# A recurrent attention and SoLU kernel on one core: chunk outputs copied aside, score matmuls in another order, masks moved

## The chip, the core and the metric

The kernel runs on one core of one Trainium2 chip. The metric is the device time in microseconds (us) of one execution. Before the change it is 380.94 us, the median of three runs (380.69 to 381.0).

## The reference

Gated linear attention over 4 batches, 8 heads, 768 steps and a head width of 48, followed by a feed-forward block over the 3072 tokens of width 384, with 1024 hidden units:

```python
for t in range(S):
    state = alpha[:, :, t, :, None] * state + np.einsum('bhd,bhe->bhde', k[:, :, t], v[:, :, t])
    y[:, :, t] = np.einsum('bhd,bhde->bhe', q[:, :, t], state)
...
h = x @ w_in
e = np.exp(h - np.max(h, axis=-1, keepdims=True))
solu = h * (e / (np.sum(e, axis=-1, keepdims=True) + 1e-09))
ln = (solu - mean) / np.sqrt(var + 1e-06) * g_ln
return (ln @ w_out).astype(np.float32)
```

`x` is `y` with its heads laid side by side; `mean` and `var` are those of `solu` along the hidden units. The weights `w_in` and `w_out` come as 64-bit floats and are converted on the chip.

## The kernel before

**Tiling.** The 768 steps are cut into six chunks of 128 (`G` = 6, numbered from 0). A chunk of all four batches is one unit of work, 512 tokens in the feed-forward block. Attention of a chunk: running products of alpha by scans on VectorE (`scan_back` L206, `scan_on` L215); keys and queries multiplied by them; scores of key against query (`scores` L271, TensorE into PSUM); the scores times a triangular mask, into `sT` in SBUF (`masked` L285, VectorE); the values read with these (`read_values` L349) on top of what the carried state gives (`read_state` L341), both into one PSUM bank per batch; a copy to `x` by ScalarE (L356). The state is decayed by GpSimd (`decay` L255, line L261) and added to (`next_state` L358).

**Rows of a head.** A head's 48 rows stand as 32 "first" rows and 16 "last" rows. The last rows of two heads share a block, so the queries of a block are copied twice by ScalarE, each time with the other head's rows at zero (`apart` L243, line L245). A score is two matmuls added in PSUM: one of first rows, one of last rows. `scores` issues, for each of four heads of a half, the first rows of four batches and then the last rows of four batches. Four banks `a0` to `a3`, one per batch, hold a half's scores; they are also used by the turned inputs, by the values and by other small products, in the order of the program.

**Feed-forward.** For each chunk `up` (L379) makes 128 hidden units at a time: three matmuls into a bank `h` (L387), Exp on ScalarE (L401), the product `h * e` on VectorE (L402), which also frees the bank, and its square on ScalarE (L403). `running` (L406) adds `e` on GpSimd and the square on VectorE (L418). `down` (L492) takes a batch of 128 tokens: eight matmuls of 385 columns into one of the two banks `o` (L498), in two halves; the last column gives the sum. `finish` (L503) computes a scale from that sum (L516 to L521 on VectorE, a power on GpSimd at L529), for chunk 0 also adds a mean (L525), scales on ScalarE (L531) and sends the rows to DRAM over SP's queue (L532).

**What sets the order.** There is no scheduler: each engine runs its instructions in the order in which the Python code issues them, and a wait holds up what stands behind it. The first part of the program is written out by hand: loads and turned inputs of chunk 0 (L670 to L695), scores and masks of chunk 0 (L696 to L702), then chunk 0's `up` steps among the conversion of the weights on VectorE (`bits` L581, lines L590 to L602, which reads what `fetch` L550 loads at L561), then chunk 0's `down` steps among the attention of chunk 1 (L742 to L812). SP's queue carries nearly all transfers, among them `move_lasts` and `move_firsts` (L227, L234), which bring queries and decays to the place where `read_state` and `decay` want them. From L816 on, a table says at which of the eight `up` steps of a chunk which part of the next chunk's attention is issued: `head` ahead of `up`, `behind` after it and ahead of `running`, `middle` after `running`, `tail` after the `down` step that is due. The table `first` holds for chunk 1's `up` steps, during which chunk 2's attention runs and no `down` is due; `usual` holds for the others.

Of the kernel before, what the change touches and what calls it, by code (L numbers as in the profile page):

```python
# [32 lines left out]
def fast_path(ctx, tc, q, k, v, alpha, moe_w_in, moe_w_out, moe_g_ln, out):  # L33
# [231 lines left out]
    def quarter(b):  # L265
        return slice(32 * b, 32 * b + 32)
# [4 lines left out]
    def scores(g, half, a=None):  # L271
        a = a or banks("a", [NP, P])
        for i in range(NP):
            h = half * NP + i
            for kb, qb in ((h, h), (H + h // 2, H + h)):
                for b in range(B):
                    nc.tensor.matmul(  # L277
                        a[b][:, i], lhsT=kT[quarter(b), kb], rhs=qv[quarter(b), qb, 0:P], start=kb == h, stop=kb != h,
                        tile_position=(32 * b, 0), skip_group_check=True,
                    )  # L280
        masks[half] = a
# [3 lines left out]
    def masked(half, batches=range(B)):  # L285
        a = masks[half]
        for b in batches:
            nc.vector.tensor_tensor(  # L288
                out=sT[:, b, half * NP : half * NP + NP], in0=a[b], in1=mask[:, None, :].to_broadcast([P, NP, P]),
                op=ALU.mult,  # L290
            )

    def keys_back(g, t=None):
# [198 lines left out]
    def down(n, half, part=range(HF)):  # L492
# [4 lines left out]
        for f in (half * HF + i for i in part):  # L497
# [3 lines left out]
            )  # L501

    def finish(n):  # L503
        g, b = divmod(n, B)
        d = st[n]
        s, o = sums[:, n], d["o"][:, 0:DM]
        t0 = b * S + g * P
        if g == G - 1:
# [6 lines left out]
            return  # L515
        nc.vector.tensor_copy(out=s[:, 0:1], in_=d["o"][:, DM : DM + 1])  # L516
        t = small.tile([P, 1], FP, name="t")
# [4 lines left out]
        if g == 0:  # L522

            o = work.tile([P, DM], FP, name="o_mean")
            nc.vector.scalar_tensor_tensor(  # L525
                out=o, in0=mean_sb, scalar=s[:, 0:1], in1=d["o"][:, 0:DM], op0=ALU.mult, op1=ALU.add
            )
        r = small.tile([P, 1], FP, name="r")
        nc.gpsimd.tensor_tensor(out=r, in0=s[:, 3:4], in1=mhalf, op=ALU.pow)  # L529
# [154 lines left out]
    scan_on(0, 0)  # L684
    t = three("tp_q", [(ps_o, "o"), (ps_o, "o"), (ps_a, "a0")])
    turned(qn, ends_of(qn, 3), t)
    for i in (2, 0, 1):
        if i == 1:
            scan_on(0, i)
        part = slice(NP * i, NP * i + NP)  # L690
        nc.vector.tensor_tensor(  # L691
            out=qe[:, :, 0:P] if i == 2 else qv[:, part, 0:P], in0=t[i], in1=aT[:, part, 1:SW], op=ALU.mult
        )
        if i == 2:
            apart()  # L695
    warm(2, ps_a, "a1")  # L696
    scores(0, 0)
    t = [x.tile([P, NP, P], FP, tag=n, name="a_" + n) for x, n in ((ps_h, "h"), (ps_o, "o")) for _ in range(2)]
    scores(0, 1, t)
    read_begin()  # L700
    masked(0)
    masked(1)  # L702
    bits(0)
# [60 lines left out]
    down(0, 1)  # L764
    mean(1)
    alpha_over(1)
    load(alpha, an, 2)
    tq += three("tp_q2", [(ps_h, "h")])
    turned(qn, ends_q, tq, range(H, NB))
    load(q, qn, 2)  # L770
    down(1, 1)
    keys_back(1, three("tp", [(ps_a, "a2"), (ps_a, "a3"), (ps_h, "h")]))
    scan_on(1, 2)
# [3 lines left out]
    move_lasts()  # L777
    finish(0)
    in_range(7)
# [6 lines left out]
    scores(1, 0)  # L786
    finish(1)
    decay(1)
    masked(0)
    down(2, 1)  # L790
    scores(1, 1)
    masked(1)
    finish(2)
    alpha_T(2)
    down(3, 0)
# [7 lines left out]
    for i in range(3):  # L803
# [5 lines left out]
    down(3, 1, (2, 3))  # L809
    finish(3)  # L810
    scan_on(2, 2)
# [10 lines left out]
    first = dict(  # L822
        head={3: "keys_back", 5: "masked0", 6: "masked1"},
        behind={0: "v", 1: "on1", 2: "lasts firsts", 3: "apart", 5: "decay", 7: "alpha back"},
        middle={7: "read1 values over"},
        tail={4: "scores0", 5: "scores1", 6: "begin read0"},
    )
# [60 lines left out]
    for g in range(1, G + 1):  # L888
# [6 lines left out]

        after = None
        if not rise:
# [520 lines left out]
```

## Time and profile before

| | |
|---|---|
| median of three runs | 380.94 us |
| the profiled execution, its own time | 380.75 us |
| its span, first to last instruction | 378.9 us |
| granted clock of TensorE, mean | 0.998 |
| busy VectorE, ScalarE, GpSimd | 246.0, 144.7, 120.5 us |
| `up` matmuls, L387 | 133.4 us |
| `down` matmuls, L498 | 133.6 us |
| score matmuls, L277 | 24.8 us, 704 records |
| value and state matmuls, L326 | 22.9 us |
| masks, L288 | 44 of 683 ns |

A page of the profile gives for each group of instructions the line, engine, operation, what is written from what, sizes and count, then busy time, the mean of one, and the idle time of the engine ahead of them with what ended it. A timeline row gives start and duration in us from the span's start, engine, line, what is written from what, and the number of records merged in the row; in brackets stands the idle time ahead of it and who ended it. PE is TensorE, PEld its loading of weights, DVE VectorE, ACT ScalarE, POOL GpSimd; SP issues transfers. A matmul of 32-bit floats leaves two records. Some matmul records are missing from a trace. A record's duration includes a tail that overlaps with the next record: where a row of many is followed at once by another, the distance between their starts tells what it cost.

### The profile page before, as it was taken

The numbers are of one execution on the slowest core, as the hardware profiler recorded it, in microseconds if no ns is written. First come the engines' busy times: TensorE is split into PE (matmuls) and PEld (weight loads), VectorE is DVE, ScalarE is ACT, GpSimd is POOL, SyncE is SP. The second block draws the span as 40 slices with busy tenths as digits, with TensorE's granted clock in tenths as the row PEclk, the third lists the DMA queues.
The fourth block names the chain that finished last, engine by engine and source line by source line (L and its number), as shares of the span: only waits on it lengthen the run. The fifth ranks groups of instructions, "written<-read, shape, count | busy, mean of one in ns | idle before, by whom it ended". The sixth has DMA issues, their size and how long they took to land. (4 is left out here: it accounts for less than half of the span.)

```text
span 378.9 us, 10022 instructions
## 1 busy us (share of the span) xinstructions
PE 362.4 (96%) x4337; PEld 215.1 (57%) x4337; DVE 246.0 (65%) x377; ACT 144.7 (38%) x256; POOL 120.5 (32%) x127
## 2 busy tenths in 40 slices
PE   8789899989999999999999999999999999999994
PEld 8675335656654665555665556565556565555552
DVE  1899878996998879855666855756965314434500
ACT  3628566681255235252341252441341142332101
POOL 7000000010246990775111765112683211333200
PEclk9999999999999999999999999999999999999999
DMA  9982968149149704836033545004041000000011
GB/s 182 189 315 89 210 205 210 43 93 194 59 107 187 172 8 98 155 87 152 22 85 76 114 104 133 24 3 106 0 112 43 24 15 8 22 22 21 27 42 49
DMA packets 72439, 36.06 MB, mean 95 GB/s; under 512 B 48184, under 2 KB 69952, under 8 KB 72384
## 3 DMA queue, kind: packets, MB, share of 16 engines
q1 hardware_dynamic: 71360, 34.39, 38.9%
q10 hardware_dynamic: 1024, 0.92, 0.7%
q8 instruction: 36, 0.59, 0.7%
q14 instruction: 19, 0.16, 0.1%
HBM read 25.30 MB, written 4.72 MB: 79 GB/s over the span
## 5 line engine op out<-in xcount | busy, mean ns | idle before, releaser
L387 PE MATMUL h<-x,w_in 128*128 128x512 f32 x288 | 133.4, 601 | 3.4 <-DVE room L402 2.1
L498 PE MATMUL o<-w_out,room 128*128 128x385 f32 x384 | 133.6, 492 | 0.9 <-DVE o_mean L525 0.9
L498 PEld LDWEIGHTS o<-w_out,room 128*128 128x128 f32 x384 | 71.1, 189 | 55.7 <-issue 13.8
L387 PEld LDWEIGHTS h<-x,w_in 128*128 128x128 f32 x288 | 52.4, 189 | 62.7 <-issue 47.7
L402 DVE TENSOR_TENSOR room<-h,e 128x512 f32<-128x512 f32 x40 | 27.6, 690 | 61.1 <-ACT e L401 61.1
L401 ACT ACTIVATE e<-h 128x512 f32<-128x512 f32 x40 | 23.8, 596 | 96.0 <-PE h L387 95.8
L418 POOL TENSOR_TENSOR p<-p,e 128x512 f32<-128x512 f32 x30 | 41.1, 1369 | 27.6 <-ACT e L401 27.2
L403 ACT ACTIVATE u<-room 128x512 f32<-128x512 f32 x40 | 25.2, 630 | 36.4 <-DVE room L402 36.4
L529 POOL TENSOR_TENSOR r<-sums,mhalf 128x1 f32<-128x1 f32 x20 | 12.2, 608 | 78.4 <-DVE sums L521 78.2
L288 DVE TENSOR_TENSOR sT<-a,mask 128x512 f32<-128x512 f32 x44 | 27.3, 683 | 14.8 <-PE a L277 14.8
L418 DVE TENSOR_TENSOR p<-p,u 128x512 f32<-128x512 f32 x30 | 24.2, 807 | 8.6 <-ACT u L403 8.6
L204 DVE TENSOR_TENSOR_SCAN hT<-aT,unit 128x516 f32<-128x516 f32 x18 | 22.3, 1285 | 7.8 <-ACT aT L674 7.7
L277 PEld LDWEIGHTS a<-qv,kT 32*128 32x128 f32 x704 | 21.9, 186 | 8.7 <-POOL p L418 1.6
L277 PE MATMUL a<-qv,kT 32*128 32x128 f32 x704 | 24.8, 278 | 1.8 <-DVE qv L691 0.8
L212 POOL COPY fend<-hT 128x12 f32<-128x12 f32 x6 | 4.1, 680 | 69.9 <-DVE hT L204 69.9
L204 DVE TENSOR_TENSOR_SCAN aT<-aT,seed 128x516 f32<-128x516 f32 x18 | 25.4, 1442 | 0.2
L326 PE MATMUL y<-sT,vn 128*32 128x128 f32 x768 | 22.9, 274 | 1.0 <-DVE sT L288 0.8
L326 PEld LDWEIGHTS y<-sT,vn 128*32 128x32 f32 x768 | 20.9, 110 | 4.3 <-issue 3.1
L225 POOL TENSOR_TENSOR kT<-kT,hT 128x1024 f32<-128x1024 f32 (+1 forms) x8 | 13.3, 1682 | 22.8 <-DVE kT L179 22.8
L196 ACT ACTIVATE sq<-an,mone 128x1536 uint8<-128x1536 f32 x12 | 18.9, 1574 | 0.2
L531 ACT ACTIVATE o_sb<-o,r 128x384 f32<-128x384 f32 x16 | 9.3, 582 | 24.1 <-POOL r L529 24.1
L356 ACT COPY x<-y 128x384 f32<-128x384 f32 x24 | 11.2, 478 | 14.4 <-PE y L326 14.2
(142 smaller groups left out, 366.0 us busy)
## 6 DMA issues: line engine op xcount, KB each, us to landing
vn<-in_v_dram SPq DMA_DIRECT2D x24, 192.0 KB, 4.3
an<-in_alpha_dram SPq DMA_DIRECT2D x20, 192.0 KB, 4.6
out_dram<-o_sb SPq DMA_DIRECT2D x20, 192.0 KB, 1.9
room<-in_moe_w_in_dram SPq DMA_DIRECT2D x6, 512.0 KB, 7.8
room<-in_moe_w_out_dram SPq DMA_DIRECT2D x8, 384.0 KB, 3.9
kn<-in_k_dram SPq DMA_DIRECT2D x16, 192.0 KB, 4.4
qn<-in_q_dram SPq DMA_DIRECT2D x16, 192.0 KB, 4.9
lot<-qe SPq DMA_DIRECT2D x40, 64.5 KB, 2.1
```

What stands on the lines that cost most here:

```text
L196: nc.scalar.activation(out=sq, in_=x, func=AF.Relu, scale=sign, bias=mone, accum_out=over[:, g, i : i + 1])
L204: nc.vector.tensor_tensor_scan(out=o, data0=a, data1=s, initial=1.0, op0=ALU.mult, op1=ALU.add)
L225: nc.gpsimd.tensor_tensor(out=kT[:, part], in0=kT[:, part], in1=hk[:, part], op=ALU.mult)
L277: nc.tensor.matmul(a[b][:, i], lhsT=kT[quarter(b), kb], rhs=qv[quarter(b), qb, 0:P], start=kb == h, stop=kb != h, tile_position=(32 * b, 0 ...
L288: nc.vector.tensor_tensor(out=sT[:, b, half * NP : half * NP + NP], in0=a[b], in1=mask[:, None, :].to_broadcast([P, NP, P]), op=ALU.mult,)
L326: nc.tensor.matmul(y_bank(b)[quarter(r), a], lhsT=lhsT, rhs=rhs, start=(b, r) not in begun, stop=stop, tile_position=(row, 32 * r), skip_g ...
L387: nc.tensor.matmul(h, lhsT=w_in[:, a, f * P : (f + 1) * P], rhs=d["x"][:, a].rearrange("p b t -> p (b t)"), start=(a == 0), stop=(a == KC ...
L401: nc.scalar.activation(out=e, in_=h, func=AF.Exp)
L402: nc.vector.tensor_tensor(out=u, in0=h, in1=e, op=ALU.mult)
L403: nc.scalar.activation(out=u2, in_=u, func=AF.Square)
L418: eng.tensor_tensor(out=p, in0=d[0][i] if f == 1 else p, in1=d[f][i], op=ALU.add)
L498: nc.tensor.matmul(d["o"][:, 0 : DM + 1], lhsT=u_of(g, f)[:, b * P : b * P + P], rhs=w_out[:, f], start=(f == 0), stop=(f == FC - 1), skip ...
```

## The change

Seven edits go together:

- **Queries in needed order.** In the prologue the query blocks are turned in the order 0 to 3, 8 to 11, 4 to 7 instead of 0 to 11, and the products follow in that order (0, 2, 1 instead of 2, 0, 1). The two warm-up matmuls ahead of the scores go; four are put ahead of the turn of the queries.
- **Scores by first rows.** `scores` issues all first rows of a half ahead of all last rows, and takes heads in the order 0, 2, 1, 3. This holds for all six chunks. Only a bank's very first matmul carries `start`.
- **Two masks off VectorE.** In chunk 0 the mask of the last batch of each half is made by a ScalarE copy from PSUM and a GpSimd product in place.
- **Copied chunks.** The outputs of chunk 0's batches 0 and 1 are copied by ScalarE from their banks into SBUF (`hold`), into a part of `lot` that is free by then; their `finish` reads the copy, and comes later: after the first and the second masks of chunk 1 instead of after `move_lasts` and after the first scores.
- **`alpha_T(2)`** is issued ahead of the second half of chunk 1's scores and masks instead of after `finish(2)`.
- **`finish(3)`** comes after the first `up` of chunk 1 instead of before the scans of chunk 2.
- **Masks ahead of a sum.** In chunk 1's `up` steps 4 and 5 the scores and masks of chunk 2 are both issued right after `up`, ahead of that step's `running`, instead of the scores at the end of the step and the masks at the head of the next.

```diff
     def scores(g, half, a=None):
         a = a or banks("a", [NP, P])
-        for i in range(NP):
-            h = half * NP + i
-            for kb, qb in ((h, h), (H + h // 2, H + h)):
+        for last in range(2):
+            for i in (0, 2, 1, 3):
+                h = half * NP + i
+                kb, qb = (H + h // 2, H + h) if last else (h, h)
                 for b in range(B):
                     nc.tensor.matmul(
-                        a[b][:, i], lhsT=kT[quarter(b), kb], rhs=qv[quarter(b), qb, 0:P], start=kb == h, stop=kb != h,
+                        a[b][:, i], lhsT=kT[quarter(b), kb], rhs=qv[quarter(b), qb, 0:P], start=not last and not i, stop=bool(last),
...
+    def masked_apart(half, b):
+
+        x = sT[:, b, half * NP : half * NP + NP]
+        nc.scalar.copy(out=x, in_=masks[half][b])
+        nc.gpsimd.tensor_tensor(out=x, in0=x, in1=mask[:, None, :].to_broadcast([P, NP, P]), op=ALU.mult)
...
+    def hold(n):
+
+        a = 2 * H * SW + (DM + 1) * (n % 2)
+        st[n]["held"] = lot[:, a : a + DM + 1]
+        nc.scalar.copy(out=st[n]["held"], in_=st[n]["o"][:, 0 : DM + 1])
+
     def finish(n):
...
-        s, o = sums[:, n], d["o"][:, 0:DM]
+        s, whole = sums[:, n], d.get("held", d["o"])
+        o = whole[:, 0:DM]
...
-    t = three("tp_q", [(ps_o, "o"), (ps_o, "o"), (ps_a, "a0")])
-    turned(qn, ends_of(qn, 3), t)
-    for i in (2, 0, 1):
+    t = three("tp_q", [(ps_a, "a0"), (ps_o, "o"), (ps_o, "o")])
+    warm(4, ps_a, "a1")
+    turned(qn, ends_of(qn, 3), t, (*range(NP), *range(H, NB), *range(NP, H)))
+    for i in (0, 2, 1):
...
-    warm(2, ps_a, "a1")
     scores(0, 0)
...
-    masked(0)
-    masked(1)
+    for half in range(2):
+        masked(half, range(B - 1))
+        masked_apart(half, B - 1)
...
     mean(1)
+    hold(0)
     alpha_over(1)
...
     down(1, 1)
+    hold(1)
     keys_back(1, three("tp", [(ps_a, "a2"), (ps_a, "a3"), (ps_h, "h")]))
...
     move_lasts()
-    finish(0)
     in_range(7)
...
     scores(1, 0)
-    finish(1)
     decay(1)
     masked(0)
+    finish(0)
+    alpha_T(2)
     down(2, 1)
     scores(1, 1)
     masked(1)
+    finish(1)
     finish(2)
-    alpha_T(2)
     down(3, 0)
...
     down(3, 1, (2, 3))
-    finish(3)
     scan_on(2, 2)
...
     first = dict(
-        head={3: "keys_back", 5: "masked0", 6: "masked1"},
-        behind={0: "v", 1: "on1", 2: "lasts firsts", 3: "apart", 5: "decay", 7: "alpha back"},
+        head={3: "keys_back"},
+        behind={
+            0: "v", 1: "on1", 2: "lasts firsts", 3: "apart", 4: "scores0 masked0", 5: "scores1 masked1 decay",
+            7: "alpha back",
+        },
+        tail={6: "begin read0"},
         middle={7: "read1 values over"},
-        tail={4: "scores0", 5: "scores1", 6: "begin read0"},
     )
...
-        after = None
+        after = 3 if g == 1 else None
```

More of the change, by code (lines that the diff above doesn't have):

```diff
@@ L515, in finish @@
             return
-        nc.vector.tensor_copy(out=s[:, 0:1], in_=d["o"][:, DM : DM + 1])
+        nc.vector.tensor_copy(out=s[:, 0:1], in_=whole[:, DM : DM + 1])
         t = small.tile([P, 1], FP, name="t")
@@ L522, in finish @@
         if g == 0:
-            o = work.tile([P, DM], FP, name="o_mean")
+            centred = work.tile([P, DM], FP, name="o_mean")
             nc.vector.scalar_tensor_tensor(
-                out=o, in0=mean_sb, scalar=s[:, 0:1], in1=d["o"][:, 0:DM], op0=ALU.mult, op1=ALU.add
+                out=centred, in0=mean_sb, scalar=s[:, 0:1], in1=o, op0=ALU.mult, op1=ALU.add
             )
+            o = centred
         r = small.tile([P, 1], FP, name="r")
```

## The prediction

> **What bounds the kernel now.** I read the page first, for which engine fills the span, then the waits of TensorE, then the timeline of TensorE around each wait, then the other engines' timelines at the same moments. The page:
>
> ```profile
> span 378.9 us, 10022 instructions
> ...
> PE 362.4 (96%) x4337; PEld 215.1 (57%) x4337; DVE 246.0 (65%) x377; ACT 144.7 (38%) x256; POOL 120.5 (32%) x127
> ```
>
> TensorE is the bound, so only its idle or slowed time can be won. Its waits, longest groups first (time, times, longest):
>
> ```profile
> PE h L387 <- DVE room L402: 2.1, 4, 0.9
> PE tp_q L164 <- DMA qn<-in_q_dram: 1.4, 1, 1.4
> ...
> PE o L498 <- DVE o_mean L525: 0.9, 1, 0.9
> PE a L277 <- DVE qv L691: 0.8, 1, 0.8
> PE y L326 <- DVE sT L288: 0.8, 1, 0.8
> ...
> PE h L387 <- DVE g_col L614: 0.7, 1, 0.7
> ```
>
> All lie before 143.2 us; from there to 373.8 us TensorE has no gap over 0.02 us. So the change can win only in the prologue (0 to 31), chunk 0's down stage (70 to 98) and chunk 1's up stage (113 to 143). Busy time hides more: TensorE's timeline in that last stage,
>
> ```profile
> 122.19 0.54 PE L277 MATMUL a<-qv,kT 32*128 32x128 f32 x8
> 123.04 2.01 PE L277 MATMUL a<-qv,kT 32*128 32x128 f32 x56 [0.32 <-ACT qv L245]
> 124.98 2.84 PE L387 MATMUL h<-x,w_in 128*128 128x512 f32 x6
> 127.76 3.44 PE L277 MATMUL a<-qv,kT 32*128 32x128 f32 x64
> 131.12 2.84 PE L387 MATMUL h<-x,w_in 128*128 128x512 f32 x6
> ```
>
> and the same 64 score records where nothing disturbs them:
>
> ```profile
> 172.65 2.07 PE L277 MATMUL a<-qv,kT 32*128 32x128 f32 x64
> 174.65 2.84 PE L387 MATMUL h<-x,w_in 128*128 128x512 f32 x6
> ```
>
> From start to next start: 2.79 and 3.36 us against 2.00. So 0.79 and 1.36 us are lost there, of which the list of waits shows 0.32.
>
> **What the Trainium skill says.** Perfetto Trace Analysis, "Identifying the Most-Contended Engine": busy matmul time is no good measure of TensorE, because its instructions overlap. The trace agrees: 3.44 against 2.07 us for equal work. PSUM — Partial Sum Buffer, "The four PSUM rules": the first matmul of a group clears written-bits of its whole bank, not data, so the new order may carry `start` on the first of a bank alone. No row prices this. GPSIMD Engine Reference, "8. Key points": it cannot read PSUM, which is why a ScalarE copy comes first. SBUF — State Buffer, "SBUF: two separate sides": a VectorE operation with two SBUF inputs and a reading GpSimd operation exclude each other. The trace agrees: L518 takes 1.29 us beside the key products, 0.16 alone. The masks have one SBUF input, and take 0.60 each.
>
> **Prologue.** Before, both query products wait for the whole turn: qe at 17.67, qv at 18.27, scan 18.87, last product 20.13. Now the first block is turned first. It is ready at about 15.9, but the scan holds VectorE to 16.80; so qv at 16.84, qe 17.45, scan 18.04, last product 19.30 to 19.99, all by 0.60 to 1.2 us a step from the old rows. ScalarE's two copies (L245) end at 18.9 and 19.5. TensorE: two warm-up matmuls (0.7 us) go from the path; four now stand in the 1.41 us wait for q, where 8 records at 0.13 plus a tail of 0.2 fit (13.4 to 14.6); were they late, the scan would hide it. First-row scores run 17.65 to 18.7, the last rows behind the copies to 20.1, the second half to 22.1. The first masks begin at 20.27 (before 21.20), three instead of four; the second half's at 22.17, so VectorE is free at 24.05 instead of 26.0.
>
> The two masks taken off it: ScalarE copy 0.6 us (as L674, 0.59), GpSimd product between 1.09 (L253) and 2.23 (the first L418 of a chunk); I take 1.29. The second ends at 24.1, at the high end 26.0 with the first queued ahead. Its reader, batch 3 of the values, comes up at 25.3: free, or 0.7 late. Values end at 26.2 (before 28.3), key turns at 27.9.
>
> This lead is not kept. The next thing on the path is VectorE's weight conversion, which sets `up` 0:
>
> ```profile
> 25.99 0.95 DVE L590 TENSOR_SCALAR lot<-room 128x768 uint32<-128x768 uint32 x1
> ...
> 29.55 0.96 DVE L602 TENSOR_TENSOR w_in<-lot 128x768 f32<-128x768 f32 x1
> 30.43 0.16 DVE L614 TENSOR_SCALAR g_col<-tp_g 128x8 f32<-128x8 f32 x1
> ```
>
> It needs three slices of w_in, and in the trace the third lands at 24.80; SP issues it at 17.39, nothing in the change moves that. So it starts at 24.85, not 24.05, and wins 25.99 - 24.85 = **1.14 us**, and TensorE waits some 1.6 us for it (27.9 to 29.5), which also covers the 0.7. From here to 82 us VectorE and ScalarE form one chain (the L402 waits) and loads follow its releases, so 1.14 is carried on. If the landing moves, so does this: I keep 0 to 1.5.
>
> **Held chunks (70 to 98), in old times less 1.14.** Two finishes leave VectorE's scan chain: each 0.97 us (82.83 - 81.86). `down(2,0)` no longer waits 0.89 for a bank; the second scores wait for L783, which ends at 85.68 instead of 86.65: TensorE gains 0.98. The two holds cost ScalarE 0.48 us each (row L356), 0.38 apart when back to back. The first delays the alpha check and with it the reload of alpha and all behind it on SP's queue by 0.4; the second delays the key copies by 0.1, which wait for TensorE anyway. Out of that queue goes one output ahead of `move_firsts` (0.6 us of issue). Net: the last move lands about 0.2 to 0.3 earlier. That matters, as the old row shows:
>
> ```profile
> 95.32 1.70 POOL L261 TENSOR_TENSOR state<-state,lot 128x384 f32<-128x384 f32 x2 [7.59 <-DMA lot<-qv]
> ```
>
> The second decay ended at 97.02, the state reads went on at 97.08. TensorE now comes at 95.3, the masks' last bank is free at 96.4 (the alpha transposes, 2.9 us, now stand ahead of the second masks), but the decay ends near 96.8. So of 0.98 + 0.31 only **0.28** stays; bounds -0.3 to 0.7. Queued behind: finishes 0 to 2 go through GpSimd after the decay, and the third's ScalarE output waits for the first output to land (issue 98.1 plus 1.9 = 100.0), with the copies of x behind it, which start at 101.5. Covered by 1 us, and by 2 more before `up` 0 would notice. The third `finish` behind `up` leaves VectorE's queue, where it took 3.2 us (106.82 to 110.05); L402 no longer makes `up` 2 wait: **0.31**.
>
> **Chunk 1's up stage.** First rows first: by my count ScalarE's copies end 0.2 and 0.6 before their scores come up, so the 0.79 goes. Masks ahead of the sum: the first masks start at TensorE's last score instead of after
>
> ```profile
> 125.50 1.19 DVE L418 TENSOR_TENSOR p<-p,u 128x512 f32<-128x512 f32 x1 [0.70 <-ACT u L403]
> 126.62 2.47 DVE L288 TENSOR_TENSOR sT<-a,mask 128x512 f32<-128x512 f32 x4
> ```
>
> They end about 0.15 before the second scores need the last bank: 1.36 goes. What is late next: the decay before the state reads. Its transfers follow twelve loads and move by 0.28 only; landing at 129.2, decay to 130.4 or 130.8. TensorE wants it at 131.46: slack 0.7. So **2.15**, bounds 1.0 to 2.2. The last wait there, 0.60 for x (L356), stays.
>
> **Sum.** 1.14 + 0.28 + 0.31 + 2.15 = 3.88 us. The profiled run took 380.75 (span 378.9 and 1.85 around it): 376.87. The median of the runs is 0.19 above it, 380.94, giving 377.06. I say 377.0. With every bound low, 0 - 0.3 + 0.31 + 1.0 = 1.0: 379.9; with every bound high, 1.5 + 0.7 + 0.31 + 2.2 = 4.7: 376.2.
>
> **Rivals.** *Gate of the weights.* The landing or VectorE's masks slip past 26.0 and the prologue gives nothing: 380.94 - 2.74 = 378.2. For it: all queues are 88% busy in the first 31 us. Against: the landing doesn't depend on the changed engines. *Gate of the decay.* In chunk 1 the transfers or GpSimd's queue, full from 120.7 to 141.4, end last, and about 1.3 of the 2.15 is given back: 378.4. For it: slack of only 0.7. Against: its products start earlier too. Both together: 379.7. *It does nothing*, because every wait is replaced: 380.9; against, the sums above would have to fail in three separate stages. *The scores themselves become slower.* Each first and last row now lie sixteen matmuls apart, in all twelve score groups; no wait covers it in the eight of chunk 1's up stage and later. At 0.49 us each the 3.88 is gone; at 0.7, 380.94 - 3.88 + 5.6 = 382.7, slower. Against: the values, also started once a bank, take 28 ns a record (3.63 / 128), the scores 31; four row groups still alternate as before.
>
> **Chances.** Forecast (376.2 to 377.8) 0.63; gate of the weights 0.11; of the decay 0.14; both 0.04; nothing 0.04; slower scores 0.04. Range 376.0 to 379.0: it leaves out both gates at once, nothing and slower, 0.12, and something at the edges. About 0.2% (0.76 us) is what a measurement can tell from no change: faster 0.92, same 0.04, slower 0.04.
>
> **What would show it.** Right: first L590 near 24.9 with VectorE idle ahead of it, `up` 0 at 29.5; a wait of about 1 us before the state reads near 95; two score groups of 2.0 us in chunk 1; no gap after about 140. Wrong: `up` 0 still near 30.6; score records over 31 ns in late chunks; state reads of chunk 1 waiting for L261; batch 3 of the values waiting for GpSimd by more than the 1.6.

## The result and the profile after

The changed kernel takes 378.33 us (median of seven runs, 377.24 to 379.79) against 380.69 us in the same session: a ratio of 0.9941, 95% interval 0.9928 to 0.9953, so faster by 2.4 us. The forecast was 377.0. Run again in a later session, unaltered, it took 377.22 us (five runs, 376.36 to 378.06), ratio 0.9902 (0.9888 to 0.9916), while the kernel before stayed at 380.7 to 381.0. Repeats of the changed kernel thus differ by more than one session's interval tells. Where variants are compared below, differences under about 1 us are read from the traces and not from the times. A trace is one execution, and shows where the time went in that one.

The profiled execution took 378.33 us. Its page:

```profile
span 376.5 us, 10033 instructions
...
PE 363.0 (96%) x4341; PEld 215.8 (57%) x4341; DVE 246.2 (65%) x375; ACT 147.1 (39%) x260; POOL 124.8 (33%) x129
```

The span is 2.36 us shorter (378.89 to 376.53 unrounded), as much as the executions differ (380.75 to 378.33). TensorE's busy time grew by 0.6 us although its work is the same but for two more warm-up matmuls, so the gain isn't seen there. Its waits, with the same columns as before:

```profile
PE h L394 <- DVE room L409: 1.6, 3, 0.9
PE h L394 <- DVE g_col L629: 1.1, 1, 1.1
...
PE y L333 <- POOL state L261: 0.9, 1, 0.9
PE y L333 <- issue: 0.6, 2, 0.5
PE h L394 <- ACT x L363: 0.6, 1, 0.6
...
PE y L333 <- DVE sT L289: 0.2, 1, 0.2
```

The waits for a bank of `down` (L525 before) and for `sums` are gone, that for the first masks fell from 0.8 to 0.2. The wait for `state` grew from 0.3 to 0.9, and "issue", time in which TensorE waited for nothing that the profile names, from 0.2 to 0.6.

The prologue, in VectorE's timeline:

```profile
23.45 0.68 DVE L289 TENSOR_TENSOR sT<-a_o,mask 128x512 f32<-128x512 f32 x1
25.18 0.95 DVE L605 TENSOR_SCALAR lot<-room 128x768 uint32<-128x768 uint32 x1 [1.05 <-DMA room<-in_moe_w_in_dram]
...
28.75 0.96 DVE L617 TENSOR_TENSOR w_in<-lot 128x768 f32<-128x768 f32 x1
29.63 0.16 DVE L629 TENSOR_SCALAR g_col<-tp_g 128x8 f32<-128x8 f32 x1
```

VectorE is free at 24.1 and then idles 1.05 us for the third slice of `w_in`. Chunk 1's up stage, in TensorE's timeline:

```profile
121.60 2.07 PE L278 MATMUL a<-qv,kT 32*128 32x128 f32 x64
123.60 2.84 PE L394 MATMUL h<-x,w_in 128*128 128x512 f32 x6
126.37 2.17 PE L278 MATMUL a<-qv,kT 32*128 32x128 f32 x64
128.47 2.84 PE L394 MATMUL h<-x,w_in 128*128 128x512 f32 x6
```

From start to next start the two score groups take 2.00 and 2.10 us, before 2.79 and 3.36.

The best way to see where the time went is to subtract the starts of the same work in the two traces, along TensorE:

| work of TensorE | before, us | after, us | earlier by | again, us | earlier by |
|---|---|---|---|---|---|
| chunk 0, first `up` | 30.66 | 29.86 | 0.80 | 29.46 | 1.20 |
| chunk 0, token sums | 66.37 | 65.45 | 0.92 | 65.22 | 1.15 |
| chunk 1, `down` between the state reads | 98.02 | 97.10 | 0.92 | 96.72 | 1.30 |
| chunk 1, `down` behind the values | 104.23 | 104.23 | **0.00** | 103.85 | **0.38** |
| chunk 2's keys turned back | 115.63 | 115.05 | 0.58 | 114.67 | 0.96 |
| chunk 2's values, then `up` | 143.16 | 140.51 | 2.65 | 140.14 | 3.02 |
| chunk 1, token sums | 147.31 | 144.98 | 2.33 | 144.73 | 2.58 |
| span | 378.89 | 376.53 | 2.36 | 376.26 | 2.63 |

("Again" is the unaltered changed kernel in the later session. "Token sums" are the matmuls `rows`, which add up a chunk's running sums for each token.) The gain is made in three places, as forecast. But in the 6 us from 98 to 104 0.92 us is lost, in the first trace all that had been won so far, and 0.3 to 0.4 us more goes just ahead of chunk 1's token sums. Nothing changes after 146.

The first loss, in TensorE's timeline of the changed kernel:

```profile
95.36 1.82 PE L333 MATMUL y<-lot,state 64*32 64x128 f32 x64 [0.87 <-POOL state L261]
97.10 1.56 PE L505 MATMUL o<-w_out,room 128*128 128x385 f32 x4
98.59 1.14 PE L333 MATMUL y<-lot,state 64*32 64x128 f32 x62
99.89 0.40 PE L333 MATMUL y<-lot,state 64*32 64x128 f32 x2 [0.15 <-issue]
100.22 4.08 PE L333 MATMUL y<-sT,vn 128*32 128x128 f32 x128
104.23 1.56 PE L505 MATMUL o<-w_out,room 128*128 128x385 f32 x4
```

and of the kernel before:

```profile
99.51 1.16 PE L326 MATMUL y<-lot,state 64*32 64x128 f32 x64
100.60 3.70 PE L326 MATMUL y<-sT,vn 128*32 128x128 f32 x128
104.23 1.24 PE L498 MATMUL o<-w_out,room 128*128 128x385 f32 x3
```

The second half of the state reads takes 1.63 us from start to next start instead of 1.09, the values 4.01 instead of 3.63: 0.54 and 0.38, together the 0.92. Only 0.15 of it has a bracket; the rest lies in the stretched rows. In single records no weights are loaded from 99.36 to 99.89 and from 103.54 to 103.89, just ahead of records 1369 and 1497 of TensorE's stream (counted from 0), 128 apart.

The second loss, in VectorE's timeline and then in GpSimd's:

```profile
139.66 4.59 DVE L204 TENSOR_TENSOR_SCAN hT<-aT,unit 128x516 f32<-128x516 f32 x3
144.17 0.66 DVE L425 TENSOR_TENSOR p<-p,u 128x512 f32<-128x512 f32 x1
```

```profile
136.25 3.63 POOL L649 TENSOR_TENSOR w_out<-w_out,mean_sb 128x384 f32<-128x384 f32 x4
139.84 2.19 POOL L425 TENSOR_TENSOR p<-p,e 128x512 f32<-128x512 f32 x1
```

Three scans take 4.59 us instead of 3.44, because GpSimd's last running sum now runs beside them; it takes 2.19 instead of 1.29. Before, that sum (140.08 to 141.37) was done before the scans began at 142.28. The step's last sum on VectorE ends at 144.83, and the token sums start at 144.98; in the later trace the list of waits names that sum as what they wait for (0.2).

### The profile page after: what moved, and what is told of

It reads as the page before. It is cut to its first block, busy times and chain, and to the rows that moved or that the text cites. A ratio compares the mean times of both kernels' runs of the same rounds, so it can differ in the third digit from the quotient of the medians.

```text
span 376.5 us, 10033 instructions
## 1 busy us (share of the span) xinstructions
PE 363.0 (96%) x4341; PEld 215.8 (57%) x4341; DVE 246.2 (65%) x375; ACT 147.1 (39%) x260; POOL 124.8 (33%) x129
## 5 line engine op out<-in xcount | busy, mean ns | idle before, releaser
L425 POOL TENSOR_TENSOR p<-p,e 128x512 f32<-128x512 f32 x30 | 42.9, 1430 | 27.2 <-ACT e L408 26.9
L425 DVE TENSOR_TENSOR p<-p,u 128x512 f32<-128x512 f32 x30 | 24.1, 804 | 7.2 <-ACT u L410 7.2
L204 DVE TENSOR_TENSOR_SCAN hT<-aT,unit 128x516 f32<-128x516 f32 x18 | 23.5, 1351 | 7.7 <-ACT aT L689 7.7
L204 DVE TENSOR_TENSOR_SCAN aT<-aT,seed 128x516 f32<-128x516 f32 x18 | 27.9, 1581 | 0.2
L278 PE MATMUL a<-qv,kT 32*128 32x128 f32 x704 | 23.8, 278 | 0.7 <-DVE qv L800 0.6
L225 POOL TENSOR_TENSOR kT<-kT,hT 128x1024 f32<-128x1024 f32 (+1 forms) x8 | 14.2, 1799 | 20.1 <-DVE kT L179 20.1
L546 ACT ACTIVATE o_sb<-o,r 128x384 f32<-128x384 f32 x16 | 9.3, 582 | 24.1 <-POOL r L544 24.1
```

The costliest lines, as they stand in the source:

```text
L204: nc.vector.tensor_tensor_scan(out=o, data0=a, data1=s, initial=1.0, op0=ALU.mult, op1=ALU.add)
L225: nc.gpsimd.tensor_tensor(out=kT[:, part], in0=kT[:, part], in1=hk[:, part], op=ALU.mult)
L278: nc.tensor.matmul(a[b][:, i], lhsT=kT[quarter(b), kb], rhs=qv[quarter(b), qb, 0:P], start=not last and not i, stop=bool(last), tile_posit ...
L425: eng.tensor_tensor(out=p, in0=d[0][i] if f == 1 else p, in1=d[f][i], op=ALU.add)
```

## The experiments

Four theories are set against each other. *Lost early gain*: what prologue and chunk 0 win is given back in chunk 1's reads, through the decay's loads and the stops without a name. *Gains add*: each part's gain reaches the end. For the stops: *instructions*, TensorE's instructions come in blocks, and a block comes late; or *something local*, such as a wait at the values that the trace doesn't name. Ratios are to the kernel before in the same session.

**Score order and table alone.** The kernel before with two of the edits.

```diff
 # in before: scores() with first rows first, and
-        head={3: "keys_back", 5: "masked0", 6: "masked1"},
+        head={3: "keys_back"},
+        behind={..., 4: "scores0 masked0", 5: "scores1 masked1 decay", 7: "alpha back"},
+        tail={6: "begin read0"},
```

> The kernel before with two of the edits alone: scores by first rows, and the table that puts chunk 2's masks ahead of the sums. Theory (the early gain is lost again before chunk 1's up stage, all that remains comes from that stage): 1.8 to 2.1 us faster than before, 378.6 to 378.9; from the start of chunk 1's up 3 to chunk 2's last value TensorE needs 2.1 us less. Rival (the gains of the parts add, as the forecast had it): the same 2.1 us, but then the other edits alone must give the missing part.

Measured: 379.68 us against 380.9, ratio 0.9968 (0.9957 to 0.9979). In the trace the stage gains 1.91 us: the reads of chunk 2's state start at 131.99 instead of 133.90, with score groups of 2.13 and 2.14 us; 1.78 is left at the token sums. The time is 1.2 us less, not the 1.8 to 2.1 expected, and the execution profiled was the fastest of the eight (378.88). These two edits give half of the change or more, and the first rows far apart don't slow the scores: in later chunks a group of 64 takes 2.07 us as before.

**The early parts alone.** The changed kernel with score order and table put back.

```diff
 # in after: scores() and the table `first` as before; the other five edits stay
```

> The changed kernel with those two edits taken back: queries in needed order, two masks off VectorE, copied chunks, moved finishes and alpha_T(2) stay. Theory: up 0 of chunk 0 starts 0.7 to 1.2 us earlier and chunk 1's scores 1.8 to 2.1 earlier, but TensorE reaches up 0 of chunk 1 with 0 to 0.3 us left; the finish taken out of VectorE's queue adds 0.5: 380.0 to 380.4 in all. Rival (gains add): 1.14 + 0.28 + 0.31 = 1.7 us, 379.0.

Measured: 380.3 us, ratio 0.9984 (0.9973 to 0.9995). The first `up` is 0.92 earlier (29.74), but at chunk 0's token sums nothing is left (66.50 against 66.37). The reason is a stop of the unnamed kind, this time in the prologue:

```profile
25.25 3.04 PE L332 MATMUL y<-sT,vn 128*32 128x128 f32 x102 [1.31 <-issue]
```

It held the values 1.31 us. The changed kernel has it too, 0.48 ahead of the same record, 478, and the kernel before 0.23 ahead of record 477. Values, copies of x and key copies came later by as much, and ScalarE's first Exp behind them at 34.61 (33.39 in the changed kernel, 34.57 in the one before). It is this Exp that chunk 0's token sums follow: they come 31.9 us after it here, 31.8 in the kernel before, 32.1 and 31.9 in the changed one's two traces. Chunk 1's second scores come 0.91 earlier, where I had 1.8 to 2.1. "Lost early gain" is borne out, "gains add" isn't, though the loss struck in another place than I had it.

**Loads of chunk 2's q later.** SP's queue asks for chunk 2's queries only behind the moves that the decay waits for.

```diff
-    load(q, qn, 2)
     down(1, 1)
...
     move_firsts()
+    load(q, qn, 2)
     down(2, 0)
```

> The changed kernel, but the reload of q for chunk 2 goes on SP's queue behind the moves of chunk 1's queries instead of ahead of them. Theory (the decay of chunk 1 waits for these moves, which wait for eight loads): the last move lands 3 to 4 us earlier, TensorE no longer waits 0.9 us ahead of the state reads, and 0.5 to 1.5 us of it reaches the end, the rest being lost to the waits named issue. Rival (TensorE is held there by its own supply of instructions, whatever the decay does): the wait moves into the issue gaps behind it, and the end stays within 0.3 us of the changed kernel.

Measured: 377.27 us, ratio 0.9911 (0.9896 to 0.9925). The last move lands at 91.65 instead of 94.96, so the decay is done before TensorE comes, and TensorE's reads are whole:

```profile
94.41 1.97 PE L333 MATMUL y<-lot,state 64*32 64x128 f32 x64
96.31 1.56 PE L505 MATMUL o<-w_out,room 128*128 128x385 f32 x4
97.81 1.16 PE L333 MATMUL y<-lot,state 64*32 64x128 f32 x64
98.90 3.70 PE L333 MATMUL y<-sT,vn 128*32 128x128 f32 x128
102.53 0.92 PE L505 MATMUL o<-w_out,room 128*128 128x385 f32 x2
```

1.09 and 3.63 us as in the kernel before, and no wait for the state: `down` starts at 102.53, 1.70 earlier than in the kernel before or the changed one, and the profiled span is 374.5. So in this trace the two unnamed stops went with the decay's wait; the combined version below has one of them without it. The times don't settle what this edit is worth by itself: its interval overlaps with that of the changed kernel's later session, and the execution profiled was the fastest of the four (376.36, the others 377.16 to 377.56).

**Outputs left out.** The rows of chunk 0's first three output tiles aren't written, one run.

```diff
-        nc.sync.dma_start(out=out[t0 : t0 + P, :], in_=o_sb)
+        if n > 2:
+            nc.sync.dma_start(out=out[t0 : t0 + P, :], in_=o_sb)
```

> The changed kernel without the three transfers that write the first three output tiles (128 rows each of batches 0 to 2), so these rows are left unwritten; everything else is as it was. It asks what stretches TensorE's gaps named issue at its records 1369 and 1497 of chunk 1's state and value reads. Theory A (the refill of TensorE's instructions is delayed by these writes, which fall on it): the refill near 97.5 is done about 0.3 us earlier and both gaps, 0.42 and 0.24, shrink under 0.1. Theory B (the refill is asked for only when TensorE is past its wait for the decay, and then takes 2.3 us or more, whatever else is moved): the gap at record 1369 stays at 0.3 to 0.6.

Measured: 377.86 us, span 376.1. The stop ahead of record 1369 stayed (99.25 to 99.79), the one ahead of 1497 went (values 3.63 us). The instruction packet before it took 0.95 us where the changed kernel's took 1.49. So the outputs don't cause the first stop. They may lengthen the second, but this run doesn't show it: in the split with the check moved, below, that stop is absent too (packet 1.03), with all outputs written.

**Instructions moved by half a block.** 46 narrow warm-up matmuls instead of 14 wide ones, 64 TensorE records more at the very start.

```diff
-    warm(14)
+    warm(46, cols=16)   # 16 columns each instead of 128
```

> The changed kernel with 46 narrow warm-up matmuls of 16 columns in place of 14 wide ones of 128 columns at its very start: 32 matmuls or 64 TensorE records more ahead of everything else[...]. Theory (TensorE's instructions come in blocks of 128 records and a late block makes the gap): the gap in the first values, ahead of record 478 in all runs so far, moves 64 records forward in the program, into the second half's first scores near 21; the values have none there. In chunk 1 gaps, if any, come 64 records earlier than records 1369 and 1497 of the changed kernel. Rival (the gap belongs to the values, through a bank or a semaphore that the trace doesn't name): it stays ahead of the same value matmul at about 23.6. The time is between 376.5 and 379.5 in both.

Measured: 391.37 us, ratio 1.0276 (1.0263 to 1.029), far outside both expectations. I had taken narrow matmuls to be short; the 92 records took 19.81 us, 0.215 each, against 0.211 for the wide ones (5.92 for 28). So TensorE's work starts 14 us late, and the time is no test of the theory. The trace is one. The stop ahead of the values in the prologue is gone, and chunk 1's reads, which here do wait 0.94 and 0.25 us for the decay, have no stop at all:

```profile
109.47 0.55 PE L333 MATMUL y<-lot,state 64*32 64x128 f32 x16 [0.94 <-POOL state L261]
110.27 1.02 PE L333 MATMUL y<-lot,state 64*32 64x128 f32 x48 [0.25 <-POOL state L261]
111.22 1.56 PE L505 MATMUL o<-w_out,room 128*128 128x385 f32 x4
112.71 1.16 PE L333 MATMUL y<-lot,state 64*32 64x128 f32 x64
113.80 3.70 PE L333 MATMUL y<-sT,vn 128*32 128x128 f32 x128
```

Same instructions, same wait, no stop: this speaks against *something local*. So does the prologue of the kernel before, which has four records fewer ahead of the values: there the stop falls 17 value records behind the wait for the mask, in the changed kernel 14, at nearly the same count of records (477 and 478). The account that is left is in the transfers that the profile names "instruction". Their packets move 16384 bytes each. In chunk 1, where the decay is waited for, a packet starts 1.0 to 1.3 us after TensorE gets past the wait (97.45 after 96.16 in the changed kernel, 95.24 after 94.19 in the split with the check moved below), and a stop ends 1.3 to 1.6 us after its packet is done (packet done 98.42, stop over 99.89; 102.47 and 103.89; in the prologue 22.81 and 24.11). In the kernel before the packet is done at 99.11 and record 1369 comes at 100.6, 1.5 later: just in time, so a reader that comes earlier has to stop unless its packet comes earlier too. Without the wait (q later) the packet was asked for at 94.71 and was early enough. With 64 records more, record 1497 lies in the middle of the values, near 115.5, 2.3 after its packet is done at 113.13. In all fourteen traces, no read or value at records 477 or 478, 1369 and 1497 starts sooner than 1.25 us after the packet ahead of it is done; where TensorE stops there for over 0.2 us, it goes on 1.25 to 1.6 after, and where it comes later than 1.6 after, it doesn't stop. What didn't come out is the expected stop 64 records earlier in the prologue: there the packet was done at 32.18, four us ahead of record 478. I did not find what decides when a packet is asked for in the prologue.

**The fetch split.** The first two pieces of `w_in` (128 hidden units each) were fetched together, in three slices of 512 KB. Now each is fetched by itself in three slices of half the size, so the first conversion waits for half the bytes.

```diff
-    fetch(0, 3, 2)
+    fetch(0, 3)
+    fetch(1, 4)
```

> The changed kernel, but the first two pieces of w_in are loaded by six transfers of one piece each instead of three of two pieces, so the first piece is complete earlier. Theory (the landing of w_in, and not the masks, now sets the start of the conversion): L605 starts at 24.1 to 24.3 instead of 25.18, up 0 of chunk 0 at 28.9 or so instead of 29.86, 0.9 us earlier, and this is carried to about 94 us, where the state reads wait for the decay; what arrives at the end is 0 to 0.9 us. Rival (the masks set it): L605 stays near 25 and nothing changes.

Measured: 377.75 us, ratio 0.9918 (0.9906 to 0.9931). The data land at 22.12, L605 starts at 23.88 right behind the masks, and the first `up` at 28.51, 1.35 earlier than in the changed kernel. At chunk 0's token sums 0.23 of it is left, because ScalarE checks the range of both pieces ahead of the first Exp, which starts at 33.37 (33.39 in the changed kernel):

```profile
31.42 0.98 ACT L593 ACTIVATE sq<-room 128x768 f32<-128x768 f32 x1
...
33.37 0.58 ACT L408 ACTIVATE sT<-h 128x512 f32<-128x512 f32 x1
```

Chunk 1's reads lose 0.37 here. In chunk 1's up stage the state reads then wait 0.70 us for the decay, which ends at 131.73: the forecast's rival *gate of the decay*. So the span, 376.7, is no shorter than the changed kernel's.

**The split, with the second check behind the first Exp.**

```diff
 # in the split version:
-    in_range(1)            # ahead of chunk 0's first up
...
+        if f == 0:
+            in_range(1)    # behind that up
```

> The split fetch of w_in with ScalarE's range check of the second piece behind chunk 0's first Exp instead of ahead of it. Theory: in the split version up 0 was 1.35 earlier but the first Exp stood behind two range checks until 33.4, which ate 1.1 of it; here the first Exp starts near 31.8, the gap of 1.6 ahead of up 3 is gone, rows(0) is at about 63.6 to 64.0 instead of 65.2, and since the decay ahead of chunk 1's state reads ends no earlier than its loads, at most 0.5 us of that reaches the end: 377.0 to 377.7. Rival: the whole 1.4 reaches the end: 376.3. Second rival: the second check then delays a later Exp as much, rows(0) stays at 65.2 and the time at 377.75.

Measured: 376.36 us, ratio 0.9886 (0.9868 to 0.9905). The first Exp starts at once:

```profile
31.20 0.19 ACT L594 ACTIVATION_READ_ACCUMULATOR sq<-sq 128x1 f32 x1
31.30 0.58 ACT L408 ACTIVATE sT<-h 128x512 f32<-128x512 f32 x1
```

Token sums of chunk 0 at 63.55, 1.9 us earlier than in the changed kernel. My theory held for this stage and fell for the next: I had the decay's loads eat all but 0.5. They follow VectorE's and ScalarE's releases, as the prediction had it, and came earlier too (decay 92.50 to 94.14 instead of 94.46 to 96.10). The span of 374.2 lies 2.1 us under that of the unaltered kernel in the same session, of which 0.38 is the stop ahead of record 1497, absent here. The medians differ by 0.9 with overlapping intervals, so the rival's 376.3 fits better, and the exact size is open.

**All eight first masks on VectorE.**

```diff
-    for half in range(2):
-        masked(half, range(B - 1))
-        masked_apart(half, B - 1)
+    masked(0)
+    masked(1)
```

> The changed kernel with all eight masks of chunk 0 on VectorE again. Theory (the landing of w_in's third slice, near 24.8 to 25.2, sets the conversion, so the two masks bought almost nothing): the masks end at 25.3 instead of 24.1, L605 starts at 25.3, at most 0.4 us later than in the changed kernel, the time 378.3 to 378.8. Rival (they are worth what they take off VectorE): 1.2 us slower, 379.5.

Measured: 377.14 us, ratio 0.9916 (0.9894 to 0.9938). VectorE's timeline:

```profile
23.80 1.27 DVE L289 TENSOR_TENSOR sT<-a_o,mask 128x512 f32<-128x512 f32 x2
24.99 0.94 DVE L605 TENSOR_SCALAR lot<-room 128x768 uint32<-128x768 uint32 x1
```

The masks end about when the slice lands (24.89), and the first `up` starts at 29.65 against 29.86 and 29.46 in the changed kernel's two traces. In this change the two masks given away bought nothing that these runs show: the time is even under the 378.3 to 378.8 that I expected.

This trace shows something else. Its span is 374.4, 2.1 us less than the changed kernel's, though chunk 0's token sums are only 0.08 earlier. In chunk 1, whose code is the changed kernel's, the last move lands at 93.89 (94.96 and 94.60 in the changed kernel's two traces), TensorE doesn't wait for the decay, and there is no stop:

```profile
94.27 1.97 PE L333 MATMUL y<-lot,state 64*32 64x128 f32 x64
...
98.75 3.70 PE L333 MATMUL y<-sT,vn 128*32 128x128 f32 x128
102.38 1.56 PE L505 MATMUL o<-w_out,room 128*128 128x385 f32 x4
```

`down` starts 1.85 earlier. So a landing about 1 us earlier went with a gain of nearly two; whether the edit or chance moved the landing is open.

**Scans of alpha behind the running sums.**

```diff
-            7: "alpha back",
+            7: "alpha",
...
-        middle={7: "read1 values over"},
+        middle={7: "back read1 values over"},
```

> The changed kernel, but in chunk 1's up step 7 the scans of alpha for chunk 3 come behind the running sum instead of ahead of it. Theory (the scans now run beside the last running sum of GpSimd and take 4.6 us instead of 3.4, so VectorE's running sum is late for the token sums): TensorE's wait of 0.34 us ahead of the token sums goes, the time 0.3 us less, 378.0. Rival (the token sums wait for GpSimd's sum, which ends at 142.0): nothing changes there, since 142.0 is long past.

Measured: 377.51 us, ratio 0.9914 (0.9899 to 0.9929). Scans and sum now meet the other way round:

```profile
138.99 0.71 DVE L425 TENSOR_TENSOR p<-p,u 128x512 f32<-128x512 f32 x1
139.59 3.47 DVE L204 TENSOR_TENSOR_SCAN hT<-aT,unit 128x516 f32<-128x516 f32 x3
```

```profile
138.94 5.23 POOL L425 TENSOR_TENSOR p<-p,e 128x512 f32<-128x512 f32 x1
```

The scans keep their 3.47 us and GpSimd's sum is drawn out to 5.23. From chunk 2's `up` to the token sums TensorE takes 4.35 us instead of 4.47 (before: 4.15). What this brings is 0.1. The lateness has changed sides: GpSimd's sum ends at 144.17, and the token sums start at 144.22. The loss between 98 and 104, in code that this edit doesn't touch, is 0.18 in this trace and not 0.92.

**All of it together**: q later, the split with the check moved, scans behind the sums.

```diff
 # in after:
-    load(q, qn, 2)         # again behind move_firsts()
-    fetch(0, 3, 2)
+    fetch(0, 3)
+    fetch(1, 4)
-    in_range(1)            # again behind the first up
-            7: "alpha back",
+            7: "alpha",        # and "back" in middle
```

> Four edits on the changed kernel together: q's reload behind the moves, w_in's first two pieces by six transfers, the range check of piece 1 behind chunk 0's first Exp, the scans behind the running sum in chunk 1's step 7. Theory: the reload's 2.0 us of span stay; with the range check out of the way the split's 1.35 us at up 0 survives by 0.6 to 1.2 us to the token sums of chunk 0; the scans give 0.3: span 371 to 373.6 against 376.5, time 373.5 to 376. Rival (each time the next wait is just behind): no more than the reload alone, 377.3.

Measured: 374.6 us (374.29 to 376.42), ratio **0.9847** (0.9824 to 0.987), faster than the changed kernel in either session. The time lies in the expected range; the profiled span, 374.05, lies above it (371 to 373.6). Two of its waits, again as time, times, longest:

```profile
PE h L394 <- DVE room L409: 1.1, 2, 0.9
...
PE y L333 <- POOL state L261: 0.6, 1, 0.6
```

The state wait is another one now: it ends at 129.09, before chunk 2's reads, where the forecast's rival *gate of the decay* had put it. In chunk 1 TensorE doesn't wait for the decay, and still one stop is there, ahead of record 1497:

```profile
96.94 4.15 PE L333 MATMUL y<-sT,vn 128*32 128x128 f32 x128
```

`down` follows at 101.02, so the values take 4.08 us instead of 3.63. The packet is done at 99.24, the stop over at 100.68, 1.44 later. So the wait isn't needed for a stop.

**The same with eight masks on VectorE.**

```diff
 # in the combined version: masked(0), masked(1) as in the kernel with eight masks above
```

> The combined version with all eight first masks back on VectorE. Theory: the two masks given to ScalarE and GpSimd bought nothing in the changed kernel because the third slice of w_in landed when VectorE was free anyway; in the combined version that slice lands near 22, so here the masks do count: the conversion at L605 starts near 25.0 instead of 23.9, up 0 of chunk 0 near 29.4 instead of 28.4, rows(0) 0.9 later, and the time is 375.4 against 374.6. Rival: VectorE has slack there in any case, or the ScalarE copies delay the first Exp as much as they help: the time is 374.6 within 0.3 and rows(0) is where it was.

Measured: 375.53 us (375.13 to 376.12), ratio 0.9856 (0.9841 to 0.987).

```profile
24.96 0.55 DVE L605 TENSOR_SCALAR lot<-room 128x768 uint32<-128x768 uint32 x1
```

against 23.93 in the combined version. The first `up` comes 0.85 later (29.23 against 28.38) and the token sums of chunk 0 0.80 later, as expected; once the landing and the range check are out of the way the two masks do count. Behind chunk 1's values 0.63 of it is left, as this version's stop ahead of record 1497 is 0.2 shorter, and the spans differ by 0.27 (374.32 and 374.05). The two times come from different sessions and their intervals overlap, so the end effect is not settled.

**The changed kernel again.**

> The changed kernel once more, unaltered, with more timed runs beside it. My theory (what is won is partly given back to waits whose length hangs on when loads land and when TensorE's instructions are refilled, and both differ from run to run): the time lies again between 377.2 and 379.8, and its trace differs from the first one only in those waits: up 0 between 29.6 and 29.9, the first value of chunk 1 between 98.9 and 100.3. Rival (the first trace shows what the kernel always does): the wait ahead of the state reads near 95 is 0.87 again, up 0 of chunk 1 starts at 105.6 again and the span is 376.5 within 0.2.

Measured: 377.22 us, ratio 0.9902 (0.9888 to 0.9916); its trace is the last pair of columns in the table above. Here the slice landed at 24.77 (25.16 the first time), L605 started at 24.79 and `up` at 29.46. The wait for the state was 0.78, the stops in chunk 1's reads took the same 0.92. The theory's range of times holds; `up` came sooner than its 29.6 to 29.9. The first value of chunk 1 (99.84) and the span (376.26) are near the first trace's, as the rival had it. But two traces don't make the 0.92 a habit: by the same subtraction the loss was 0.18 with the scans moved and nothing with eight masks, with the same code in that stretch, and 0.37 to 0.61 in four other traces that wait for the decay.

## Why the prediction was right, and where it wasn't

The sum of the forecast against the two traces, in us:

| term | forecast | first trace | again |
|---|---|---|---|
| prologue, carried to the end of chunk 0's up stage | 1.14 | 0.92 | 1.15 |
| held chunks, to the `down` between the state reads | 0.28 | 0.00 | 0.15 |
| state reads and values of chunk 1 | none | **-0.92** | **-0.92** |
| third `finish` moved | 0.31 | 0.58 | 0.58 |
| chunk 1's up stage | 2.15 | 2.07 | 2.06 |
| ahead of chunk 1's token sums | none | -0.32 | -0.44 |
| sum, to those token sums | 3.88 | 2.33 | 2.58 |

**Prologue.** The size came out, the mechanism in part. Scores came at 17.73 (forecast 17.65), the first mask at 20.34 (20.27), VectorE was free at 24.13 (24.05), then idle until the slice lands. ScalarE's copies took 0.59, GpSimd's products 1.27 and 1.28 (1.29 taken), the second ended at 24.32 and the values didn't wait for it. The 24.80 for the landing was one trace's number; 25.16 and 24.77 were seen after. That moved the first `up`'s gain between 0.80 and 1.20, inside the bounds of 0 to 1.5. But the first `up` isn't what is carried on. ScalarE's first Exp stands behind the values, the copies of x and of the keys, and two range checks; before and after:

```profile
34.57 0.58 ACT L401 ACTIVATE sT<-h 128x512 f32<-128x512 f32 x1
```

```profile
33.39 0.58 ACT L408 ACTIVATE sT<-h 128x512 f32<-128x512 f32 x1
```

The Exp came 1.18 earlier since the values did (the last one at 26.88 instead of 28.06). Where `up` alone came earlier, 0.92 in the early parts alone and 1.35 with the split, the token sums gained nothing and 0.23. So "This lead is not kept", said of the values, was wrong: it was the lead that counted, and that it was about as large as the conversion's 1.14 was luck. It was smaller than forecast, too: the values ended at 27.15 and not 26.2, with a stop of 0.48 among them.

**Held chunks.** The wait for the bank went and the scores of chunk 1 came 1.85 earlier (84.85 instead of 86.70). TensorE then waited for the decay, 0.87 + 0.15 us, as forecast ("about 1 us near 95"). The decay gained no more than the prologue gave it in the first trace. The 0.28 was small and near its low side.

**The step that failed** is the one behind it: that what is left at the state reads, 1.14 and 0.28, goes on to the end ("So of 0.98 + 0.31 only **0.28** stays" has no term behind it for TensorE's own stream). The runs showed 0.92 us of stops in TensorE's own stream between 98 and 104, in both traces of the changed kernel. The row that could have warned me was in the profile before, "y L326 <- issue: 0.2": I passed over it as small. The Trainium skill, Runtime: NRT & Kernel Launch, "Instruction fetch mechanics", says that instructions are refilled in blocks of 256 (16 KiB) while the engine executes the current one, and that crossing a block is "mostly hidden". The traces agree on the block, with packets of 16384 bytes and stops 128 records apart (a record and its load of weights are two instructions). Here it wasn't hidden: 0.2 to 1.3 us a stop, in streams of short matmuls of 17 to 28 ns a record. Shown is that the stops keep to a count of records and to the end of a packet, and that their size differs from trace to trace of the same code. That late packets are their cause rests on this order of times in fourteen traces and is not shown by taking away the packets.

**Third `finish`.** Forecast from the 0.31 that the list of waits showed; it gave 0.58. Direction right, size under.

**Chunk 1's up stage.** Right within 0.1 in both traces, and the edit by itself gives 1.91. The decay was later than forecast, 129.58 to 131.23 in the changed kernel instead of ending by 130.8, since its last move landed at 129.85 and not near 129.2. It didn't hold the reads at 131.25, but little of the slack of 0.7 was left. The rival *gate of the decay* came true with the split (a wait of 0.70) and in the two combined versions (0.62 and 0.58). *Slower scores* did not: 2.07 us a group of 64 at 170 and 178 us, the same as before.

**Ahead of the token sums.** The forecast said "no gap after about 140", meaning that nothing would be lost there. A gap of 0.13 stands at 144.98 and 0.32 goes in all. VectorE's scans start 2.62 us earlier (139.66 instead of 142.28), GpSimd's last sum behind its centring of `w_out` only 0.24 (139.84 instead of 140.08), so the two now meet. The Trainium skill's SBUF — State Buffer, "SBUF: two separate sides", already quoted in the forecast, says that such a pair excludes each other; the trace agrees (4.59 for 3.44, 2.19 for 1.29). I had applied it to one place and not to the rest of the queue. That this pair is the whole of the loss isn't shown: with the scans moved 0.12 came back, and GpSimd's sum was late instead.

That the median still fell in the range owes something to its width: with the two unforeseen losses, 3.88 becomes about 2.6, and the range up to 379.0 had been kept for gates of this size, if others. One sum of the forecast is off: both gates together come to 379.5 by its own terms, not 379.7.

## What to carry to other kernels

Carry a gain along the path from stage to stage and ask at each what else is due at that moment, since a stage that was on time by accident takes the gain back: here record 1369 already came only 1.5 us after its instructions, and of the 0.92 by which TensorE came earlier nothing was left two stops on. Where two engines gate a stage, follow both before crediting one with the gain. Read small "issue" waits in streams of short matmuls as a resource with its own due times, and look at the instruction packets beside the engine's waits. When an edit frees an engine, check that its next input has landed before pricing the edit: the two masks bought nothing until the fetch was split and the range check moved.

## What the runs showed of the hardware that I had not expected

- Warm-up matmuls of 16 columns took as long as those of 128: 0.215 against 0.211 us a record, all into one bank from one stationary operand.
- TensorE stood 0.2 to 1.3 us, waiting for nothing that the profile names, in the middle of a stream of short matmuls: ahead of the same few records wherever it did, with the stop ending 1.25 to 1.6 us after a packet of instructions was done.
- The landing of one and the same load, issued at the same place of the queue, differed between executions by 0.4 us at 25 us (24.77 and 25.16), and that alone moved the first `up` by 0.4. Chunk 0's token sums moved by 0.23.
- A running sum of GpSimd (1.27 us elsewhere, at 134.96) took 5.23 us when it was started ahead of VectorE's three scans, while the scans kept their 3.47; started 0.18 us after the first scan, it took 2.19 and the scans 4.59.
